# An MLP backward kernel: derivative operations placed one by one by a plan with a clock per engine, a denser warm-up, a tail split over two engines, and thirty extra matmuls at the end

## The chip, the cores and the metric

One core of a Trainium2 chip. The metric is the device time of one execution in microseconds (us); lower is better. A run is repeated, and the runs of the kernel before are taken on the same chip, in the same rounds. The profile is one execution. Its span is about 2 us shorter than the timed figure.

Names: PE is TensorE (matmul), PEld its weight load, DVE VectorE, ACT ScalarE, POOL GpSimd, SP SyncE, which issues most DMAs here. A name with a q (ACTq, SPq) is the sequencer that issues DMAs. The granted clock (PEclk in the views) is the share of its full clock that PE is allowed in a stretch of time.

## The reference

```python
# x [1,2048,448], w1 [448,1792], b1, w2 [1792,448], b2, grad_out [1,2048,448]; all bf16
def fwd(x, w1, b1, w2, b2):
    h = gelu_tanh(x @ w1 + b1)
    return h @ w2 + b2
out, vjp = jax.vjp(fwd, x, w1, b1, w2, b2)
return out, *vjp(grad_out)          # out, dx, dw1, db1, dw2, db2
```

The kernel does this in four stages. With z = x @ w1 + b1:

1. **Forward**: 28 steps (4 blocks of 512 rows, 7 column pairs each). A step has a first product (8 matmuls, z into PSUM), an evacuation pair on ScalarE (gelu into `hT`, a copy of z into `Z`), and a second product (8 matmuls from `hT`, out into four PSUM banks).
2. **Gradient of w2**: 14 groups of 16 matmuls, each evacuated by ScalarE into `gw2_t`.
3. **Backward**: again 28 steps. The evacuation, on VectorE, multiplies by the derivative of gelu, which must stand in `Z` by then.
4. **Gradient of w1**: dense matmuls, little else.

The derivative of gelu is elementwise work on `Z`, 28 pairs of tiles of 128x1024: s (square), v (polynomial), tanh on ScalarE, y, n, and E, the sum. It fills the gaps of VectorE and ScalarE in stages 1 to 3. In the *early* form y uses `hT` while it is still there; in the *late* form `hT` is gone, and s and one more square run on ScalarE.

## The kernel before

The queue of an engine is worked off in the order in which instructions were emitted. `Background` decides that order for the derivative work by credit: each step grants each engine some microseconds, and operations are emitted while credit lasts.

```python
class Background:
    def step(self, dve, act):
        for e, c in (("V", dve), ("A", act)):
            self.credit[e] = min(self.credit[e] + c, 4.0)
        ...  # while anything moved:
        for e in ("V", "A"):
            q = self.ops[e]
            if q and self.credit[e] > 0 and (q[0][3] is None or q[0][3] in self.done):
                cost, fn, tag, _ = q.pop(0)
                fn()                     # emits the instruction(s)
                self.credit[e] -= cost
                self.done.add(tag)       # "done" means emitted
```

A tanh may therefore be emitted in the same step as the v that it reads.

```python
# forward, step p (cut)
pair_mms(ps, w1_sb, xq, fts)                                  # first product
nc.scalar.activation(out=hT[:], in_=ps[:], func=ACT.Gelu_apprx_tanh)
nc.scalar.activation(out=Z[b][...], in_=ps[:], func=ACT.Identity)
chain_step(accs[pb], hist[p - 1], w2_sb, pc)                  # second product of step p-1
if pc == NPAIR - 1:
    out_rows(pb, accs[pb], out2, True)                        # o_blk: 4 additions on VectorE
    dve -= 2.8
bg.step(dve, STEP - 2.16)
...
# gradient of w2 (cut)
gw2_t = tmp.tile([P, 2, D], BF16, name="gw2_t")               # two buffers
nc.scalar.copy(out=gw2_t[:, h, :], in_=ps_w[:, 0:D])
bg.step(3.03, 3.03 - 0.55)                                    # one per 16 matmuls of 3.03 us
...
# backward, step p (cut)
nc.vector.scalar_tensor_tensor(out=ghT[:, h, :], in0=Z[b][:, ft, :], ..., in1=ps[:, h, :], ...)
chain_step(accs[pb], hist[p - 1], w1T_sb, pc)
```

Of the kernel before, what the change touches and what calls it, by code (L numbers as in the profile page):

```python
# [19 lines left out]
def kernel(  # L20
# [49 lines left out]
    class Background:  # L70
        def __init__(self):
            self.ops = {"V": [], "A": []}
            self.done = set()
            self.credit = {"V": 0.0, "A": 0.0}

        def add(self, eng, cost, fn, tag=None, after=None):
            self.ops[eng].append((cost, fn, tag, after))

        def step(self, dve, act):
            for e, c in (("V", dve), ("A", act)):  # L80
                self.credit[e] = min(self.credit[e] + c, 4.0)
            moved = True
            while moved:
                moved = False
                for e in ("V", "A"):
                    q = self.ops[e]
                    if q and self.credit[e] > 0 and (q[0][3] is None or q[0][3] in self.done):
                        cost, fn, tag, _ = q.pop(0)
                        fn()
                        self.credit[e] -= cost  # L90
                        self.done.add(tag)
                        moved = True

        def need(self, tag):
            while tag not in self.done and (self.ops["V"] or self.ops["A"]):
                self.step(1.0, 1.0)

    bg = Background()

    def emit_E(b, c, hT, k, prevs, s_on_act):  # L100
        zc = Z[b][:, 2 * c:2 * c + 2, :]
        t = {}

        def new(nm):
            t[nm] = tmp.tile([P, 2, SB], BF16, name=nm)
            return t[nm]

        def s_():
            s = new("s")
            if s_on_act:  # L110
                nc.scalar.activation(out=s[:], in_=zc, func=ACT.Square)  # L111
            else:
                nc.vector.tensor_tensor(out=s[:], in0=zc, in1=zc, op=ALU.mult)

        def u_():
            v = new("v")
            nc.vector.tensor_scalar(out=v[:], in0=t["s"][:], scalar1=GELU_A, scalar2=1.0, op0=ALU.mult, op1=ALU.add)  # L117
            nc.vector.tensor_tensor(out=v[:], in0=v[:], in1=zc, op=ALU.mult)  # L118

        def tanh_():  # L120
            nc.scalar.activation(out=t["v"][:], in_=t["v"][:], func=ACT.Tanh, scale=GELU_C)  # L121

        def y_():
            y = new("y")
            f = 2.0 if hT is not None else 1.0
            nc.vector.tensor_scalar(out=y[:], in0=t["s"][:], scalar1=f * 3.0 * GELU_A * GELU_C, scalar2=f * GELU_C, op0=ALU.mult, op1=ALU.add)
            nc.vector.tensor_tensor(out=y[:], in0=y[:], in1=zc if hT is None else hT[:], op=ALU.mult)

        def sq_():
            n = new("n")  # L130
            nc.scalar.activation(out=n[:], in_=t["v"][:], func=ACT.Square)  # L131

        def E_():
            if hT is None:
                n = t["n"]
                nc.vector.tensor_scalar(out=n[:], in0=n[:], scalar1=-1.0, scalar2=1.0, op0=ALU.mult, op1=ALU.add)
            else:
                n = new("n")
                nc.vector.tensor_scalar(out=n[:], in0=t["v"][:], scalar1=-1.0, scalar2=1.0, op0=ALU.mult, op1=ALU.add)
            nc.vector.tensor_tensor(out=t["y"][:], in0=t["y"][:], in1=n[:], op=ALU.mult)  # L140
            nc.vector.tensor_tensor(out=zc, in0=t["y"][:], in1=t["v"][:], op=ALU.add)

        if s_on_act:
            bg.add("A", 1.09, s_, ("s", k))
        else:
            bg.add("V", 0.69, s_, ("s", k))
        bg.add("V", 1.12, u_, ("u", k), ("s", k))
        bg.add("A", 1.09, tanh_, ("t", k), ("u", k))
        if hT is None:
            bg.add("A", 1.09, sq_, ("q", k))  # L150
        bg.add("V", 1.12, y_, ("y", k), ("u", k))
        prevs.append((1.81, E_, ("E", b, c), ("q", k) if hT is None else ("t", k)))
        while len(prevs) > 1:
            cost, fn, tag, after = prevs.pop(0)
            bg.add("V", cost, fn, tag, after)
# [19 lines left out]
    pw = [psum_acc.tile([P, SB], F32, name="acc") for _ in range(3)]  # L175
    for i in range(5):
        nc.tensor.matmul(pw[0][:], lhsT=warm[:, 0:P], rhs=warm[:, 0:SB], start=True, stop=True)
    H = P // 2
    for i in range(3):
        for r in range(2):  # L180
            rs = slice(r * H, (r + 1) * H)
            nc.tensor.matmul(pw[1 + r][:, 0:256], lhsT=warm[rs, 0:P], rhs=warm[rs, 0:256], start=True, stop=True)
    for i in range(2):
        for r in range(2):
            rs = slice(r * H, (r + 1) * H)
            for q in range(2):
                nc.tensor.matmul(pw[1 + r][q * H:(q + 1) * H, 0:256], lhsT=warm[rs, q * H:(q + 1) * H], rhs=warm[rs, 0:256],
                                 start=True, stop=True, skip_group_check=True)
# [39 lines left out]
    def out_rows(b, acc, dst, with_b2):  # L228
        blk = tmp.tile([P, SPB, D], BF16, name="o_blk", tag="rows")
        for j in range(SPB):  # L230
            if with_b2:
                nc.vector.tensor_tensor(out=blk[:, j, :], in0=acc[j][:, 0:D], in1=b2_bc[:], op=ALU.add)  # L232
            else:
                nc.scalar.mul(out=blk[:, j, :], in_=acc[j][:, 0:D], mul=0.5)  # L234
        nc.gpsimd.dma_start(out=dst[b * SB:(b + 1) * SB, :].rearrange("(j p) d -> p j d", p=P), in_=blk[:])  # L235

# [4 lines left out]
    STEP = 3.24  # L241
    g_all = big.tile([P, NS, D], BF16, name="g_all", tag="nat_d")
    steps = [(b, c) for b in range(NB) for c in range(NPAIR)]
    late = []
    prevs = []
    accs = {}
    hist = []
    for p in range(len(steps) + 1):
        if p < len(steps):
# [5 lines left out]
            pair_mms(ps, w1_sb, xq, fts)  # L255
            hT = tmp.tile([P, 2, SB], BF16, name="hT", bufs=6)
            nc.scalar.activation(out=hT[:], in_=ps[:], func=ACT.Gelu_apprx_tanh)  # L257
            transpose_out(h_nat, hT, b, fts)
            nc.scalar.activation(out=Z[b][:, 2 * c:2 * c + 2, :], in_=ps[:], func=ACT.Identity)
# [4 lines left out]
            hist.append(hT)  # L264
        dve = STEP
        if p > 0:
            pb, pc = steps[p - 1]
            if pc == 0:
                accs[pb] = [psum_acc.tile([P, SB], F32, name="acc") for _ in range(SPB)]
            chain_step(accs[pb], hist[p - 1], w2_sb, pc)  # L270
            if pc == NPAIR - 1:
                out_rows(pb, accs[pb], out2, True)
                dve -= 2.8
            if pc % 2 == 0:
                emit_E(pb, pc, hist[p - 1], p - 1, prevs, False)
            else:
                late.append((pb, pc))
        bg.step(dve, STEP - 2.16)

# [8 lines left out]
    for k, (b, c) in enumerate(late):  # L288
        emit_E(b, c, None, 100 + k, prevs, True)
    if prevs:  # L290
        bg.add("V", *prevs.pop(0))
# [16 lines left out]
    for st in range(1, NS):  # L308
        bg.add("V", 0.65, lambda st=st: gsum_op(st), ("gsum", st))

    out4_v = out_4.rearrange("(ft p) d -> p ft d", p=P)
    for c in range(NPAIR):
        gw2_t = tmp.tile([P, 2, D], BF16, name="gw2_t")
        for h in range(2):
            ft = 2 * c + h
            ps_w = psum_acc.tile([P, 512], F32, name="acc")
            for st in range(NS):
                nc.tensor.matmul(ps_w[:, 0:D], lhsT=h_nat[:, st, ft * P:(ft + 1) * P], rhs=g_all[:, st, :],  # L318
                                 start=(st == 0), stop=(st == NS - 1))
            nc.scalar.copy(out=gw2_t[:, h, :], in_=ps_w[:, 0:D])  # L320
            bg.step(3.03, 3.03 - 0.55)
# [3 lines left out]
    hist = []  # L325
    for p in range(len(steps) + 1):
        if p < len(steps):
# [4 lines left out]
            bg.need(("E", b, c))  # L332
            ps = psum_z.tile([P, 2, SB], F32, name="ps")
            pair_mms(ps, w2T_sb, gq, fts)
            ghT = tmp.tile([P, 2, SB], BF16, name="hT", bufs=6)
            for h, ft in enumerate(fts):
                nc.vector.scalar_tensor_tensor(out=ghT[:, h, :], in0=Z[b][:, ft, :], scalar=1.0, in1=ps[:, h, :], op0=ALU.add, op1=ALU.mult,  # L337
                                               accum_out=gb1_p[:, b, ft:ft + 1])
            transpose_out(gh_nat, ghT, b, fts)
            if c == 1 and b + 1 < NB:  # L340
                gq_n = load_T(g2, b + 1, "gT_q")
            hist.append(ghT)
        if p > 0:
# [3 lines left out]
            chain_step(accs[pb], hist[p - 1], w1T_sb, pc)  # L347
            if pc == NPAIR - 1:
                out_rows(pb, accs[pb], gx2, False)
        bg.step(STEP - 1.4, STEP - 0.5)  # L350
    assert not bg.ops["V"] and not bg.ops["A"]
# [19 lines left out]
    for cp in range(NCH // 2):  # L371
# [19 lines left out]
        nc.scalar.mul(out=tl[:], in_=ps_w[:, 0:CW], mul=0.5)  # L391
        for h in range(2):
            cs = slice((2 * cp + h) * CW, (2 * cp + h + 1) * CW)
            nc.sync.dma_start(out=out_2[(KD - 1) * P:D, cs], in_=tl[h * DL:(h + 1) * DL, :])


# [28 lines left out]
```

## Time and profile before

| | before |
|---|---|
| time, median | 298.11 us (3 runs, 297.99 to 298.87) |
| span of the profiled run | 295.5 us |
| PE busy | 276.4 us, 94% |
| VectorE, ScalarE busy | 175.9 us, 128.1 us |

PE is the bottleneck, so the question is where it idles or runs slowly. The profile page gives the first hint: the busy tenths of PE, and of its granted clock, in 40 slices of the span.

```profile
PE   7999979989998999998955999999999999999994
PEclk9999999999999999999995999999999999999999
```

Slices 21 and 22 (148 to 163 us, the start of backward) are about half empty, and slice 22 also has a lower clock. The timeline of PE gives sizes. Its columns are start, duration, engine and line, operation, how many, and in brackets the idle time just before and what ended it.

```profile
5.57 5.66 PE L163 MATMUL ps<-xT_q,w_sb 128*128 128x512 bf16 x16 [0.72 <-DMA xT_q<-in_x_dram]
37.45 1.69 PE L170 MATMUL acc<-w_sb,hT 128*128 128x448 bf16 x8 [0.30 <-ACT hT L257]
42.10 1.69 PE L170 MATMUL acc<-w_sb,hT 128*128 128x448 bf16 x8 [1.23 <-ACT hT L257]
...
135.82 12.27 PE L318 MATMUL acc<-g_all,h_nat 128*128 128x448 bf16 x64 [1.12 <-ACT gw_t L320]
158.76 3.17 PE L170 MATMUL acc<-w1T_sb,hT 128*128 128x448 bf16 x8 [7.22 <-DVE hT L337]
```

Read from the top: the first 16 matmuls take 5.66 us (16 of the same kind take 3.62 us at 147.92); twice in each of three blocks PE waits for ScalarE's gelu evacuation; it waits twice (0.19 and 1.12 us) for a bank that ScalarE should have emptied; and it waits 7.22 us for VectorE when backward starts, after which 8 matmuls take 3.17 us instead of the usual 1.68.

Why the evacuation was late: ScalarE's timeline around the first block boundary (L121 is tanh, L257 gelu, L259 the copy of z).

```profile
35.43 1.06 ACT L121 ACTIVATE v<-v 128x1024 bf16<-128x1024 bf16 x1 [2.78 <-DVE v L118]
36.39 1.00 ACT L257 ACTIVATE hT<-ps 128x1024 bf16<-128x1024 f32 x1
37.30 1.01 ACT L259 ACTIVATE Z_103<-ps 128x1024 bf16<-128x1024 f32 x1
40.08 1.06 ACT L121 ACTIVATE v<-v 128x1024 bf16<-128x1024 bf16 x1 [1.76 <-DVE v L118]
41.04 1.00 ACT L257 ACTIVATE hT<-ps 128x1024 bf16<-128x1024 f32 x1
```

Tanh stood at the head of the queue for 2.78 us, waiting for VectorE, and the gelu that PE needed stood behind it. The Trainium skill, "TensorE: Matmul & The Clock Gate", Part 1 (Engine queue depths), calls these queues "strict FIFO"; this trace agrees: the gelu at 36.39 starts as the tanh ends (35.43 plus 1.06 us), though its input had been ready since about 33.9.

Why VectorE was late in backward: VectorE's timeline just before its first evacuation (L337).

```profile
152.63 0.43 DVE L117 TENSOR_SCALAR v<-s 128x1024 bf16<-128x1024 bf16 x1 [0.30 <-ACT s L111]
156.94 0.43 DVE L117 TENSOR_SCALAR v<-s 128x1024 bf16<-128x1024 bf16 x1 [0.30 <-ACT s L111]
157.40 0.69 DVE L118 TENSOR_TENSOR v<-v,Z_105 128x1024 bf16<-128x1024 bf16 x1
158.01 0.68 DVE L337 SCALAR_TENSOR_TENSOR hT<-Z_102,ps 128x512 bf16<-128x512 bf16 x1
```

One derivative pair takes 4.31 us here (156.94 minus 152.63), and the first evacuation, whose input had been ready since about 150 us, stands behind them.

The end of the span: the last real matmuls, the last evacuation and its two DMA issues.

```profile
288.20 3.22 PE L388 MATMUL acc<-gh_nat,x_all 128*64 128x448 bf16 x32
291.51 0.54 ACT L391 ACTIVATE gw_tail<-acc 128x448 bf16<-128x448 f32 x1 [2.66 <-PE acc L388]
292.08 1.11 SPq L394 DMA_DIRECT2D out_dram<-gw_tail  x2
```

### The profile page before, as it was taken

The numbers are of one execution on the slowest core, as the hardware profiler recorded it, in microseconds if no ns is written. First come the engines' busy times: TensorE is split into PE (matmuls) and PEld (weight loads), VectorE is DVE, ScalarE is ACT, GpSimd is POOL, SyncE is SP. The second block draws the span as 40 slices with busy tenths as digits, with TensorE's granted clock in tenths as the row PEclk, the third lists the DMA queues.
The fourth block names the chain that finished last, engine by engine and source line by source line (L and its number), as shares of the span: only waits on it lengthen the run. The fifth ranks groups of instructions, "written<-read, shape, count | busy, mean of one in ns | idle before, by whom it ended". The sixth has DMA issues, their size and how long they took to land.

```text
span 295.5 us, 3804 instructions
## 1 busy us (share of the span) xinstructions
PE 276.4 (94%) x1396; PEld 133.3 (45%) x1396; DVE 175.9 (60%) x362; ACT 128.1 (43%) x153; POOL 22.0 (7%) x31
## 2 busy tenths in 40 slices
PE   7999979989998999998955999999999999999994
PEld 2444434434443455544522444444444444555552
DVE  1366799599599799859999889933433442000000
ACT  1677478568749738669887202002002002211211
POOL 0002100100010011200000001061000001000000
PEclk9999999999999999999995999999999999999999
DMA  7997967576453499941003654869775664211111
GB/s 200 318 162 186 272 122 111 106 151 126 92 133 71 91 170 236 209 84 63 31 31 69 124 105 93 169 115 289 164 120 106 152 91 106 78 49 31 35 45 31
DMA packets 99844, 36.46 MB, mean 123 GB/s; under 512 B 92145, under 2 KB 97889, under 8 KB 99826
## 3 DMA queue, kind: packets, MB, share of 16 engines
q1 hardware_dynamic: 96352, 26.81, 48.0%
q0 software_dynamic: 2512, 8.95, 10.1%
q10 hardware_dynamic: 962, 0.46, 0.6%
q8 instruction: 11, 0.18, 0.3%
q14 instruction: 7, 0.06, 0.1%
HBM read 7.00 MB, written 6.89 MB: 47 GB/s over the span
## 4 chain that ended last, share of the span: by engine, by line
PE 69%; ACT 9%; DVE 9%; DMA 8%; issue 3%; SPq 1%; POOL 1%; ACTq 0%; POOLq 0%; DVEq 0%
PE ps L163 27%; PE acc L170 25%; PE acc L378 12%; DMA out_dram<-gw_t 3%; ACT v L121 3%; DVE v L118 2%; ACT s L111 2%; DVE o_blk L232 2%; PE acc L388 2%; PE acc L318 2%; DVE v L117 2%; ACT hT L257 2%; DMA h_nat<-hT 2%; DMA xT_q<-in_x_dram 2%; DMA w2T_sb<-in_w_dram 2%
## 5 line engine op out<-in xcount | busy, mean ns | idle before, releaser
L170 PEld LDWEIGHTS <-hT 128*128 128x128 bf16 x448 | 43.6, 99 | 58.1 <-DVE hT L337 7.7
L163 PE MATMUL ps<-xT_q,w_sb 128*128 128x512 bf16 x224 | 54.8, 390 | 0.7 <-DMA xT_q<-in_x_dram 0.7
L170 PE MATMUL acc<-w1T_sb,hT 128*128 128x448 bf16 x224 | 48.3, 360 | 7.2 <-DVE hT L337 7.2
L163 PE MATMUL ps<-gT_q,w2T_sb 128*128 128x512 bf16 x224 | 53.6, 383 | 0.0
L170 PE MATMUL acc<-w_sb,hT 128*128 128x448 bf16 x224 | 46.8, 353 | 4.5 <-ACT hT L257 4.5
L318 PE MATMUL acc<-g_all,h_nat 128*128 128x448 bf16 x224 | 42.9, 352 | 1.3 <-ACT gw_t L320 1.3
L121 ACT ACTIVATE v<-v 128x1024 bf16<-128x1024 bf16 x28 | 29.6, 1058 | 32.1 <-DVE v L118 32.1
L234 ACT ACTIVATE o_blk<-acc 128x448 bf16<-128x448 f32 x16 | 7.4, 550 | 72.8 <-issue 40.0
L378 PE MATMUL acc<-gh_nat,x_all 128*128 128x448 bf16 x192 | 36.8, 353 | 0.0
L163 PEld LDWEIGHTS <-w_sb 128*128 128x128 bf16 x224 | 22.4, 100 | 27.5 <-issue 3.6
L257 ACT ACTIVATE hT<-ps 128x1024 bf16<-128x1024 f32 x28 | 28.5, 1018 | 13.9 <-PE ps L163 13.7
L163 PEld LDWEIGHTS <-w2T_sb 128*128 128x128 bf16 x224 | 22.2, 99 | 25.9 <-issue 1.5
L318 PEld LDWEIGHTS <-h_nat 128*128 128x128 bf16 x224 | 21.9, 98 | 22.1 <-issue 1.8
L378 PEld LDWEIGHTS <-x_all 128*128 128x128 bf16 x192 | 18.6, 98 | 17.6 <-issue 0.4
L140 DVE TENSOR_TENSOR y<-y,n 128x1024 bf16<-128x1024 bf16 x28 | 19.4, 692 | 1.0
L382 ACT ACTIVATE gw_t<-acc 128x448 bf16<-128x448 f32 x12 | 6.5, 543 | 29.9 <-PE acc L378 27.6
L337 DVE SCALAR_TENSOR_TENSOR hT<-Z_104,ps 128x512 bf16<-128x512 bf16 x14 | 9.1, 685 | 13.6 <-PE ps L163 13.6
L337 DVE SCALAR_TENSOR_TENSOR hT<-Z_105,ps 128x512 bf16<-128x512 bf16 x14 | 9.1, 685 | 13.5 <-PE ps L163 13.5
L117 DVE TENSOR_SCALAR v<-s 128x1024 bf16<-128x1024 bf16 x28 | 12.9, 461 | 7.0 <-ACT s L111 6.3
L235 POOL DMA_DIRECT2D out_dram<-o_blk x8 | 6.1, 761 | 129.3 <-ACT o_blk L234 75.6
L232 DVE TENSOR_TENSOR o_blk<-acc,b_bc 128x448 bf16<-128x448 f32 x16 | 8.9, 617 | 10.7 <-PE acc L170 10.7
L131 ACT ACTIVATE n<-v 128x1024 bf16<-128x1024 bf16 x12 | 12.7, 1057 | 0.4
(70 smaller groups left out, 208.9 us busy)
## 6 DMA issues: line engine op xcount, KB each, us to landing
out_dram<-o_blk POOLq DMA_DIRECT2D x8, 448.0 KB, 3.9
g_all<-in_grad_out_dram POOLq DMA_DIRECT2D x1, 1792.0 KB, 10.2
x_all<-in_x_dram POOLq DMA_DIRECT2D x1, 1792.0 KB, 9.8
out_dram<-gw_t POOLq DMA_DIRECT2D x7, 224.0 KB, 2.5
out_dram<-gw_t SPq DMA_DIRECT2D x12, 112.0 KB, 1.7
w_sb<-in_w_dram SPq DMA_DIRECT2D x1, 896.0 KB, 6.9
h_nat<-hT SPq DMA_TRANSPOSE x56, 2.5
gh_nat<-hT SPq DMA_TRANSPOSE x56, 2.5
```

The source lines that it names most:

```text
L117: nc.vector.tensor_scalar(out=v[:], in0=t["s"][:], scalar1=GELU_A, scalar2=1.0, op0=ALU.mult, op1=ALU.add)
L121: nc.scalar.activation(out=t["v"][:], in_=t["v"][:], func=ACT.Tanh, scale=GELU_C)
L131: nc.scalar.activation(out=n[:], in_=t["v"][:], func=ACT.Square)
L140: nc.vector.tensor_tensor(out=t["y"][:], in0=t["y"][:], in1=n[:], op=ALU.mult)
L163: nc.tensor.matmul(ps[:, h, :], lhsT=lhs[:, kt, ft * P:(ft + 1) * P], rhs=rhs[:, kt, :], start=(kt == 0), stop=(kt == KD - 1))
L170: nc.tensor.matmul(acc[j][:, 0:D], lhsT=lhs[:, h, j * P:(j + 1) * P], rhs=w[:, ft, :], start=(ft == 0), stop=(ft == NF - 1))
L232: nc.vector.tensor_tensor(out=blk[:, j, :], in0=acc[j][:, 0:D], in1=b2_bc[:], op=ALU.add)
L234: nc.scalar.mul(out=blk[:, j, :], in_=acc[j][:, 0:D], mul=0.5)
L257: nc.scalar.activation(out=hT[:], in_=ps[:], func=ACT.Gelu_apprx_tanh)
L318: nc.tensor.matmul(ps_w[:, 0:D], lhsT=h_nat[:, st, ft * P:(ft + 1) * P], rhs=g_all[:, st, :], start=(st == 0), stop=(st == NS - 1))
L337: nc.vector.scalar_tensor_tensor(out=ghT[:, h, :], in0=Z[b][:, ft, :], scalar=1.0, in1=ps[:, h, :], op0=ALU.add, op1=ALU.mult, accum_out=g ...
L378: nc.tensor.matmul(ps_w[:, 0:CW], lhsT=x_all[:, st, kt * P:(kt + 1) * P], rhs=gh_nat[:, st, cs], start=(st == 0), stop=(st == NS - 1))
```

## The change

Intent: emit each derivative operation alone, in a gap that ends before the next due evacuation, by a plan that keeps one clock per engine; and warm PE up with denser work. The core of the diff, cut:

```diff
-    class Background:            # credit per step
+    class Plan:
+            self.t = {"P": 6.0, "A": 6.0, "V": 6.0}      # a clock per engine
+            self.end, self.bg, self.due = ...            # end times by tag; waiting ops; when the next evacuation is due
+        def fill(self):
+            while True:
+                # among the ops whose inputs have a planned end: the earliest start,
+                # if it also ends by the time the engine's next evacuation is due
+                if k and k[0] + self.bg[e][k[1]][0] <= self.due[e] and (...):
+        def fg(self, eng, cost, fn, tag=None, after=0.0, slack=0.3):
+            if eng != "P":
+                self.due[eng] = after + slack
+                self.fill()
+            fn()
+            self.t[eng] = max(self.t[eng], after) + cost
...
-        bg.add("V", 1.12, u_, ("u", k), ("s", k))        # two VectorE instructions in one entry
+        plan.add("V", 0.44, u_, ("u1", k), (("s", k),))  # one instruction per entry
+        plan.add("V", 0.70, u2_, ("u", k), (("u1", k),))
...
-            if pc % 2 == 0:      # 16 early pairs, 12 late ones
-                emit_E(pb, pc, hist[p - 1], p - 1, prevs, False)
+            open_ = [e for e in early if ("y",) + e not in plan.end]
+            if len(open_) < 3:   # as many early pairs as get through: 18, and 10 late ones
+                early.append((b, c))
+                emit_E(b, c, hT)
...
-    for i in range(5):           # warm-up: 5 full matmuls, then 6 and 8 on part of the array
-        nc.tensor.matmul(pw[0][:], lhsT=warm[:, 0:P], rhs=warm[:, 0:SB], start=True, stop=True)
-    ...
+    for i in range(10):          # 10 full matmuls
+        nc.tensor.matmul(pw[:], lhsT=warm[:, 0:P], rhs=warm[:, 0:SB], start=True, stop=True)
...
         tl = tmp.tile([P, CW], BF16, name="gw1_tail", tag="rows")
-        nc.scalar.mul(out=tl[:], in_=ps_w[:, 0:CW], mul=0.5)
         for h in range(2):
-            nc.sync.dma_start(out=out_2[(KD - 1) * P:D, cs], in_=tl[h * DL:(h + 1) * DL, :])
+            if h == 0:
+                nc.scalar.mul(out=tl[hs, :], in_=ps_w[hs, 0:CW], mul=0.5)
+                nc.scalar.dma_start(out=out_2[(KD - 1) * P:D, cs], in_=tl[hs, :])
+            else:
+                nc.vector.tensor_scalar(out=tl[hs, :], in0=ps_w[hs, 0:CW], scalar1=0.5, ...)
+                nc.sync.dma_start(out=out_2[(KD - 1) * P:D, cs], in_=tl[hs, :])
+    # after everything: 30 matmuls on half the rows, in pairs, into banks that nothing reads
+    for lo, ro, acc_ in ((0, 0, 0), (0, 0, 1), (0, 1, 0), (1, 0, 0), (1, 1, 1)):
+        for i in range(3):
+            for r, bank in enumerate((pa, pb_)):
+                nc.tensor.matmul(bank, lhsT=x_all[HS[r], ...], rhs=gh_nat[HS[r], ...], ...)
```

The work on the data is the same, apart from two pairs that change from the late to the early form.

## The prediction

> **What bounds it.** TensorE. The page gives PE 94% busy; the span is 295.5 us (298.1 us timed). I read PE's losses from its timeline, idle intervals and matmuls slower than steady state (8 first-product matmuls 1.73 us, 8 second-product ones 1.51 us, so 3.24 us a step):
>
> - Start: the first 16 real matmuls take 5.66 us, not 3.46: 2.2 us lost.  The Trainium skill, "TensorE: Matmul & The Clock Gate", Part 1, says the array is at half clock until about 3.4 us of sustained work fill a free-running window. The warm-up of before is thin (small tiles) and leaves 0.72 us idle.
> - Forward: six waits of PE for the hT evacuation on ScalarE, 0.3 and 1.23 us per block boundary, 4.5 us in all, and 1.1 us of restarts. The chain of waits names the cause: o_blk on VectorE holds up v, tanh heads ScalarE's queue waiting for v (2.75 us), and the evacuation stands behind tanh.
> - w2 gradient: 1.3 us of waits for free banks.
> - Backward start: PE idles 7.22 us (151.5 to 158.8) since VectorE still works off derivative operations, then 2.4 us more at granted clock 0.5. Together 9.6 us.
>
> Sum: 18.9 us. Without it the matmuls need about 267 us of the 285.9 between first and last.
>
> **What the change does.** The built order shows tanh no longer ahead of an evacuation it would delay: after each o_blk three evacuation pairs precede the next tanh. 18 pairs instead of 16 take the cheap form, so Square runs on ScalarE 10+10 times instead of 12+12. The gsum additions (15 x 0.65 us) move from before the first backward evacuation to the third backward block. VectorE's total, about 176 us, hardly changes; it is full in forward but no longer blocks PE.
> Warm-up: 10 full matmuls, at the trace's cold rate (about 0.43 us) 1.2 to 5.5 us, just up to x's arrival at 5.57, dense.
> Tail: two evacuations and two DMA issues in parallel save one issue, 0.55 us. The 30 probe matmuls after the last real one use half the rows; if pairs overlap, as the six half-row warm-up matmuls of before did (0.82 us, 1.28 if serial), 15 x 0.22 = 3.3 us fits under the 3.6 us of evacuation and output DMA; if they don't, 6.5 us, costing 3.
> x_all's load now starts after gsum, about 7 steps (24 us) before it is needed; 2.9 us reduction and 9.8 us landing fit.
>
> **Sum.** Start -1.7, forward -5.0, w2 gradient -1.0, backward start -9.2, tail -0.4: -17.3 us. Predicted 280.8 us, 8 in 10 between 278.8 and 283.8; faster by over 2% 0.97, within 2% 0.02, slower 0.01.
>
> **What would show it.** Chain of waits almost wholly PE; PE idle before hT waits under 1 us in forward; no idle over 1 us at backward start and no 0.5 clock there; first 16 matmuls at 3.5 to 4.5 us; gw_t waits for its DMA (3.9 us) may stay, as the slow first output behind the w2T memset is unchanged, and delay the derivative chain by up to 8 us, which four banks and VectorE's slack should absorb. Last matmul to end of span: about 3.6 us.
>
> **What would make it wrong.** That 8 us delay, unknown to the plan, could leave 1 to 4 us idle at backward start; probe pairs may serialise (+3); x_all may arrive late; the clock window's phase moves the start by 1 us.

## The result

| | before | changed |
|---|---|---|
| time, median | 298.05 us (4 runs, 296.38 to 298.87) | 282.0 us (4 runs, 281.53 to 284.11) |
| span of the profiled run | 295.5 us | 280.1 us |
| PE busy | 94% | 98% |

The ratio is 0.9482, with a 95% interval from 0.9419 to 0.9546. Ratios here are the mean time of one kernel's fast runs over that of the other's of the same rounds, so not quite the ratio of the medians that are quoted.

PE's slices on the page of the changed kernel are full from the third to the last but one; the page has no clock row, since no change of clock was recorded.

```profile
PE   7799999999999999999999999999999999999998
```

All the idle times of PE that its timeline lists (line numbers are those of the changed file: L200 is the first product, L207 the second, L214 the warm-up):

```profile
1.21 4.45 PE L214 MATMUL acc<-warm 128*128 128x512 bf16 x10 [1.21 <-DVE warm L211]
5.87 2.40 PE L200 MATMUL ps<-xT_q,w_sb 128*128 128x512 bf16 x8 [0.20 <-DMA xT_q<-in_x_dram]
9.04 0.82 PE L200 MATMUL ps<-xT_q,w_sb 128*128 128x512 bf16 x3 [0.77 <-DMA w_sb<-in_w_dram]
10.99 1.25 PE L200 MATMUL ps<-xT_q,w_sb 128*128 128x512 bf16 x5 [1.13 <-DMA w_sb<-in_w_dram]
```

After 11 us the timeline lists nothing: no wait for gelu, for a bank, or for VectorE. (It leaves out the shortest ones; the page has 0.1 us before L354, the gradient of w2, which matters in experiment 6.) At the first block boundary ScalarE now reads (L154 tanh, L298 gelu, L300 the copy of z):

```profile
31.72 1.02 ACT L298 ACTIVATE hT<-ps 128x1024 bf16<-128x1024 f32 x1 [0.36 <-PE ps L200]
32.64 1.02 ACT L300 ACTIVATE Z_92<-ps 128x1024 bf16<-128x1024 f32 x1
34.96 1.02 ACT L298 ACTIVATE hT<-ps 128x1024 bf16<-128x1024 f32 x1 [1.30 <-PE ps L200]
...
40.02 1.06 ACT L154 ACTIVATE v<-v 128x1024 bf16<-128x1024 bf16 x1
```

Gelu waits for PE, and not PE for gelu; the next tanh comes three evacuation pairs later, without waiting. VectorE's first backward evacuation now waits for PE as well:

```profile
143.95 0.69 DVE L382 SCALAR_TENSOR_TENSOR hT<-Z_91,ps 128x512 bf16<-128x512 bf16 x1 [1.87 <-PE ps L200]
```

The tail of the changed kernel: last real matmuls, the extra ones (L448) and the two evacuations.

```profile
272.66 3.22 PE L429 MATMUL acc<-gh_nat,x_all 128*64 128x448 bf16 x32
275.81 3.41 PE L448 MATMUL ps<-gh_nat,x_all 64*128 64x512 bf16 x30
275.97 0.54 ACT L436 ACTIVATE gw_tail<-acc 64x448 bf16<-64x448 f32 x1 [2.66 <-PE acc L429]
276.54 0.63 DVE L439 TENSOR_SCALAR gw_tail<-acc 64x448 bf16<-64x448 f32 x1 [20.79 <-ACT gw_tail L436]
```

VectorE's half waits for ScalarE's half, so they do not run side by side.

Where the time came from, by stage, from the starts of the first matmul of each stage in the two timelines. (The second product's first matmul ends "start"; the last boundary is the end of the last real matmul, 291.44 and 275.88 us in the chain of waits, the profile's view that follows the work that ended last back through what released each step.)

| stage | before | changed | difference | predicted |
|---|---|---|---|---|
| start, up to the first second product | 11.07 | 12.08 | +1.0 | -1.7 |
| rest of forward | 92.84 | 87.26 | -5.6 | -5.0 |
| gradient of w2 | 44.01 | 42.68 | -1.3 | -1.0 |
| backward | 100.36 | 90.72 | -9.6 | -9.2 |
| gradient of w1 | 43.16 | 43.14 | 0.0 | |
| last real matmul to end of span | 4.06 | 4.22 | +0.2 | -0.4 |
| span | 295.5 | 280.1 | -15.4 | -17.3 |

The three stages in the middle came as predicted. The start and the tail did not, and both got slower instead of faster. So there were two questions for experiments: which part of the plan earns the 16 us, and what holds the start and the tail.

### The profile page after: what moved, and what is told of

Same layout as the page of the kernel before. It is cut to its first block, busy times and chain, and to the rows that moved or that the text cites. A ratio compares the mean times of both kernels' runs of the same rounds, so it can differ in the third digit from the quotient of the medians.

```text
span 280.1 us, 3825 instructions
## 1 busy us (share of the span) xinstructions
PE 274.9 (98%) x1400; PEld 134.5 (48%) x1417; DVE 170.4 (61%) x366; ACT 124.5 (44%) x149; POOL 22.0 (8%) x31
## 4 chain that ended last, share of the span: by engine, by line
PE 89%; DMA 8%; SPq 1%; POOL 1%; issue 0%; ACT 0%; ACTq 0%; POOLq 0%
PE ps L200 33%; PE acc L207 30%; PE acc L419 13%; PE acc L354 9%; DMA w_sb<-in_w_dram 3%; DMA out_dram<-gw_t 3%; PE acc L429 2%; DMA w2T_sb<-in_w_dram 2%; PE ps L448 1%; SPq L318 1%; POOL w2T_sb L320 1%; ACT gw_t L356 0%; ACTq L224 0%; PE ps L406 0%; POOLq L320 0%
## 5 line engine op out<-in xcount | busy, mean ns | idle before, releaser
L207 PEld LDWEIGHTS <-hT 128*128 128x128 bf16 x448 | 43.8, 98 | 43.8
L200 PE MATMUL ps<-xT_q,w_sb 128*128 128x512 bf16 x216 | 52.8, 382 | 2.4 <-DMA w_sb<-in_w_dram 1.9
L200 PE MATMUL ps<-gT_q,w2T_sb 128*128 128x512 bf16 x215 | 52.0, 379 | 0.5
L207 PE MATMUL acc<-w_sb,hT 128*128 128x448 bf16 x224 | 46.8, 352 | 0.1
L207 PE MATMUL acc<-w1T_sb,hT 128*128 128x448 bf16 x224 | 46.8, 352 | 0.0
L354 PE MATMUL acc<-g_all,h_nat 128*128 128x448 bf16 x224 | 42.7, 352 | 0.1
L154 ACT ACTIVATE v<-v 128x1024 bf16<-128x1024 bf16 x28 | 29.6, 1059 | 21.5 <-DVE v L151 21.4
L298 ACT ACTIVATE hT<-ps 128x1024 bf16<-128x1024 f32 x28 | 28.7, 1024 | 22.5 <-PE ps L200 18.1
L200 PEld LDWEIGHTS <-w_sb 128*128 128x128 bf16 x224 | 21.9, 99 | 28.6 <-DMA w_sb<-in_w_dram 2.9
L200 PEld LDWEIGHTS <-w2T_sb 128*128 128x128 bf16 x224 | 21.9, 98 | 25.0
L354 PEld LDWEIGHTS <-h_nat 128*128 128x128 bf16 x224 | 21.9, 98 | 20.8 <-issue 0.4
L439 DVE TENSOR_SCALAR gw_tail<-acc 64x448 bf16<-64x448 f32 x2 | 1.3, 628 | 39.6 <-ACT gw_tail L436 39.6
L148 DVE TENSOR_SCALAR v<-s 128x1024 bf16<-128x1024 bf16 x28 | 12.2, 434 | 8.2 <-ACT s L144 7.8
L356 ACT CAST gw_t<-acc 128x448 bf16<-128x448 f32 x14 | 7.2, 532 | 21.7 <-PE acc L354 12.5
L382 DVE SCALAR_TENSOR_TENSOR hT<-Z_94,ps 128x512 bf16<-128x512 bf16 x14 | 9.1, 685 | 12.4 <-PE ps L200 12.4
L170 DVE TENSOR_SCALAR n<-v 128x1024 bf16<-128x1024 bf16 x18 | 8.9, 493 | 12.2 <-ACT v L154 12.2
```

The source lines that it names most:

```text
L148: nc.vector.tensor_scalar(out=v[:], in0=t["s"][:], scalar1=GELU_A, scalar2=1.0, op0=ALU.mult, op1=ALU.add)
L154: nc.scalar.activation(out=t["v"][:], in_=t["v"][:], func=ACT.Tanh, scale=GELU_C)
L170: nc.vector.tensor_scalar(out=n[:], in0=src[:], scalar1=-1.0, scalar2=1.0, op0=ALU.mult, op1=ALU.add)
L200: nc.tensor.matmul(ps[:, h, :], lhsT=lhs[:, kt, ft * P:(ft + 1) * P], rhs=rhs[:, kt, :], start=(kt == 0), stop=(kt == KD - 1))
L207: nc.tensor.matmul(acc[j][:, 0:D], lhsT=lhs[:, h, j * P:(j + 1) * P], rhs=w[:, ft, :], start=(ft == 0), stop=(ft == NF - 1))
L298: h_end[p] = plan.fg("A", 1.05, lambda: nc.scalar.activation(out=hT[:], in_=ps[:], func=ACT.Gelu_apprx_tanh), after=m1_end + LAT)
```

## The experiments

Twelve kernels, all with correct results. Times are medians of all runs; each ratio is against the kernel before in the same rounds and leaves slow runs out. The kernel before had 299.42 us in the rounds of the first four (7 runs, three of them slow; 298.47 without these), 297.71 in those of the next four (11 runs, two slow; 297.35 without) and 298.51 in those of the last four (11 runs, none slow). The three sets ran on three chips. The record calls the class of each of the first four runs "unclear", so what is read from those four rests on their traces as much as on their ratios.

### 1. Only the place of tanh (b_lag)

On the kernel before: a tanh may be emitted only if its v was emitted in an earlier step, in forward alone.

```diff
+            old = set(self.done)          # what was emitted before this step
-                    if q and self.credit[e] > 0 and (q[0][3] is None or q[0][3] in self.done):
+                    if q and self.credit[e] > 0 and (q[0][3] is None or q[0][3] in (old if self.lag and e == "A" else self.done)):
...
+    bg.lag = False                        # after forward
```

> The kernel before, with one rule added in the forward stage: a tanh may be emitted only in the step after the one that emitted its input v, so at least one more evacuation pair stands ahead of it. Theory (tanh waiting at the head of ScalarE's queue causes the forward stalls): PE waits for hT in forward fall from 4.5 us to under 1 us, their 1.1 us of restarts go as well, the backward start keeps its idle time of about 7 us; 298.0 becomes about 292.5 (ratio 0.98). Rival (the forward stalls come from VectorE being full, and will return wherever tanh stands): PE waits of 3 us or more stay in forward, ratio 0.99 to 1.0.

Measured: 294.93 us, ratio 0.9898 (0.9833 to 0.9962). The forward waits are gone altogether, as the theory has it: the next idle time of PE after the start comes at 123 us. The sum is not what I expected. PE's timeline at the start of backward:

```profile
142.34 3.62 PE L165 MATMUL ps<-gT_q,w2T_sb 128*128 128x512 bf16 x16
155.83 3.17 PE L172 MATMUL acc<-w1T_sb,hT 128*128 128x448 bf16 x8 [9.88 <-DVE hT L340]
```

Backward's first matmul is 5.6 us earlier than before (147.92), but VectorE was not freed by as much, so the idle time there grew from 7.22 to 9.88 us. Nearly half of what forward won was handed to the next wait.

### 2. Only the place of the first backward evacuation (b_credit)

On the kernel before: less credit for VectorE during the gradient of w2, so that 22 pairs stand ahead of the first evacuation instead of 25. No operation changes.

```diff
-            bg.step(3.03, 3.03 - 0.55)
+            bg.step(2.15, 3.03 - 0.55)
```

> The kernel before, with VectorE's credit per half pair of the w2 gradient cut from 3.03 to 2.15, so that 22 derivative pairs instead of 25 stand in VectorE's queue ahead of the first backward evacuation; same work, same form, other place. Theory (place, not amount, causes the idle time at the start of backward): the idle time of 7.2 us and the half clock after it vanish, ratio 0.968 (about 288.5). Rival (VectorE or the pair chain is simply behind): the wait returns in the first two backward blocks where the same pairs come due, ratio 0.985 or more.

Measured: 288.37 us, ratio 0.9671 (0.9612 to 0.9731). This is the theory's number, and the wait for VectorE did not come back: in backward PE's timeline lists only this, after the first block.

```profile
174.61 2.41 PE L170 MATMUL acc<-w1T_sb,hT 128*128 128x448 bf16 x8 [0.66 <-ACT o_blk L234]
```

The same work in another place is worth 9.8 us by the ratio and 8.3 us in the profiled runs (spans of 295.5 and 287.2 us). VectorE was not too slow for its work; three pairs too many stood ahead of the one instruction that PE needed.

### 3. Both together (b_lag_credit)

> Both edits on the kernel before. Theory (the two stalls are separate and local, and the plan with clocks adds nothing else of size): savings add up, 5.5 plus 9.6, about 283 us, ratio 0.949, the time of the changed kernel. Rival (18 cheap pairs, single operations in gaps and the interleaving matter by themselves): 286 us or more, ratio 0.96 or more.

Measured: 284.17 us (283.5 to 284.39), ratio 0.9525 (0.9474 to 0.9575). Two local edits to the kernel before, without a plan, without single operations and with 16 early pairs, reach all but about 2 us of the changed kernel (1.9 us between the profiled spans; the intervals of the two ratios overlap). My expectation was 283 us, 0.949; the measured value lies between the two theories. The traces show what is missing. Both kernels reach the first second product at 12.08 us. Then:

```profile
123.96 3.19 PE L321 MATMUL acc<-g_all,h_nat 128*128 128x448 bf16 x16 [0.24 <-ACT gw_t L323]
127.37 15.29 PE L321 MATMUL acc<-g_all,h_nat 128*128 128x448 bf16 x80 [0.22 <-ACT gw_t L323]
169.46 2.40 PE L172 MATMUL acc<-w1T_sb,hT 128*128 128x448 bf16 x8 [0.66 <-ACT o_blk L236]
```

The first matmul of the gradient of w1 starts at 234.78 us here and at 232.74 in the changed kernel, 2.04 us apart. The three waits (1.1 us) and the 0.7 us by which the last line's eight matmuls exceed their usual 1.68 make up 1.8 of those 2 us. All three lines wait for a ScalarE evacuation. Which ingredient of the plan removes them (single operations, due times, or the 18 early pairs) was not separated.

### 4. Was a slow DMA the root of the late VectorE? (b_bufs)

On the kernel before, four `gw2_t` buffers. With two, ScalarE waits 3.9 us for the first output of this stage to land, and VectorE 3.4 us for ScalarE.

```diff
-        gw2_t = tmp.tile([P, 2, D], BF16, name="gw2_t")
+        gw2_t = tmp.tile([P, 2, D], BF16, name="gw2_t", bufs=4)
```

> The kernel before, with four gw2_t buffers instead of two, so ScalarE no longer waits 3.9 us for the slow first output of the w2 gradient and VectorE no longer 3.4 us for s. Theory (25 pairs ahead of the first backward evacuation are too many even so): the idle time at the start of backward falls from 7.2 to about 3.8 us, with or without the half clock after it; the waits of 1.3 us for banks go; ratio 0.975 to 0.985. Rival (this wait is the root of the late VectorE): the idle time vanishes, ratio 0.965 or less.

Measured: 295.59 us, ratio 0.9929 (0.9851 to 1.0007). The waits for banks went, so PE reached backward 1.3 us earlier (146.58), and the wait for VectorE only fell to 6.23 us:

```profile
156.43 3.17 PE L170 MATMUL acc<-w1T_sb,hT 128*128 128x448 bf16 x8 [6.23 <-DVE hT L337]
```

The rival (this DMA is the root) is out. The theory's direction holds, its size was too large: VectorE came 2.3 us earlier, not 3.4. Its pairs keep their spacing of 4.31 us even when ScalarE does not wait, because VectorE itself is busy for about 4.0 of these.

### 5 to 7. The start: warm-up against load order (a_oldwarm, a_load, a_load_oldwarm)

The changed kernel's warm-up worked as such: its ten matmuls and the first three real ones are about 0.4 us apart, and from 7.03 us on (5.8 us after the first) the real ones run at the short spacing, about 0.22 us. But PE then waits for w1 (0.77 and 1.13 us in the timeline above). I took two edits. One puts the old warm-up back. The other moves columns 256 to 511 of w1 to the queue that loads x, right behind x:

```diff
-    load_w1(nc.scalar, 256, 512)
+    load_w1(nc.sync, 256, 512)
     load_w2(nc.sync, 0, 2)
     load_w1(nc.sync, 512, 1024)
```

On the other queue the issue of these two pieces waited for the landing of earlier ones (in the changed kernel they were issued at 3.97 and 5.62 us). The Trainium skill, "DMA: Bandwidth & Descriptors", section "Queues, rings and completion order", says that within a queue, on each DMA engine, descriptors are consumed in ring order; so what is issued first on the busy queue should be served first. The outcome agrees: in a_load the two pieces were issued at 3.57 and 4.20 us and landed 3.1 and 2.7 us later, while in the changed kernel the second one took 5.3 us.

> The changed kernel with the warm-up of before. Theory W (at the start the third and fourth pieces of w1, which land near 11 us, bound the first 16 matmuls once PE is warm, so the longer warm-up only turns half clock into waiting): same time as the changed kernel within 0.6 us, first second-product matmul at 11 to 12.2 us. Rival, the step of the prediction (the warm-up saves 1.7 us): 1.7 us slower than the changed kernel, 283.7 against 282.0.

> The changed kernel with w1 columns 256 to 511 issued on the queue of x, right behind x and ahead of w2 and the rest of w1, instead of on the other queue where the issue waits for an earlier landing. Theory W: the waits of PE for w1 (1.9 us) go, the first second-product matmul starts 1.5 to 2 us earlier than 12.1, about 280.3 us, ratio 0.943. Rival (the DMA engines are full until 11 us, whatever the order): within 0.5 us of the changed kernel.

> The same load order with the warm-up of before. Theory W: now that w1 is early, the clock bounds the start, and the old warm-up costs 1 to 2 us against the new load order with the new warm-up. Rival (the warm-up is worth nothing in any case): same within 0.5 us.

The first entry is from the changed kernel's own rounds, the other three share their rounds. Times are medians of all runs; one of a_load's six is slow (285.51), and its fast ones alone have 280.83.

| | warm-up new | warm-up old |
|---|---|---|
| old load order | 282.0 us, 0.9482 (changed kernel) | 281.87 us, 0.9480 (a_oldwarm) |
| new load order | 281.46 us, 0.9448 (a_load) | 282.81 us, 0.9502 (a_load_oldwarm) |

First, with the old load order the new warm-up is worth nothing that shows. The two ratios agree, though their intervals (0.9419 to 0.9546 and 0.9444 to 0.9516) alone would not exclude 1.7 us; the traces decide. The first second product starts at 12.08 us with the new and at 12.23 with the old one, and both wait for the same piece of w1, to 10.99 (above) and to 11.14 us (a_oldwarm):

```profile
11.14 1.25 PE L200 MATMUL ps<-xT_q,w_sb 128*128 128x512 bf16 x5 [1.02 <-DMA w_sb<-in_w_dram]
```

That is where the predicted 1.7 us went: the faster clock only makes PE wait for the next piece.

Second, the new load order does move the start: the first second product begins at 9.66 us instead of 12.08 in the profiled run, with no wait for w1 listed:

```profile
5.62 4.20 PE L200 MATMUL ps<-xT_q,w_sb 128*128 128x512 bf16 x16
```

Yet the whole kernel gained only about 1 us (fast runs: 280.83 against a_oldwarm's 281.87), and the profiled run, one of the two longer fast ones, only 0.2 us of span against the changed kernel's. PE's timeline of a_load shows where 2.35 of the 2.4 us went in it, and the chain of waits (start, duration, what) leads there:

```profile
106.19 1.32 SPq L318
107.55 4.90 DMA w2T_sb<-in_w_dram
112.58 1.53 POOL w2T_sb L320
114.12 8.85 DMA out_dram<-gw_t
```

```profile
123.65 18.32 PE L354 MATMUL acc<-g_all,h_nat 128*128 128x448 bf16 x96 [2.35 <-ACT gw_t L356]
```

The load of w2 transposed, the memset on POOL behind it, and the first `gw2_t` output behind that on POOL's queue are a chain that hardly moves with PE's start: that output lands at 123 us in the changed kernel too. There PE waits only about 0.1 us for the bank, yet the chain of waits of the changed kernel already runs through it:

```profile
114.49 8.69 DMA out_dram<-gw_t
123.86 18.32 PE acc L354 x96
```

So the changed kernel had no slack left here. Whoever makes its PE faster before 123 us runs into this limit, and the 1.7 us forecast for the start would have done so too.

Third, that new wait can also cost the clock. In the profiled run of a_load_oldwarm it was 2.10 us, and PE's clock halved right after it (columns of the windows: stretch, length, PE busy and count, granted clock, DMA share, GB/s):

```profile
120.00:122.00 2.00, 1.57 (x9) 1.00 1.15 241
122.00:124.00 2.00, 0.34 (x2) 0.93 1.34 173
124.00:126.00 2.00, 2.00 (x7) 0.50 0.80 186
```

In a_load's profiled run a wait of 2.35 us at the same place was not followed by it. The Trainium skill, "TensorE: Matmul & The Clock Gate", Part 1, describes a free-running window of about 3.4 us. The recorded stretch at half clock lasted 3.41 us, one such window; why the shorter wait was enough and the longer one was not, no run here shows. Three of a_load_oldwarm's six runs had a mean clock of 0.994, as one such stretch would give, and those are its longer ones (283.69 to 285.06 against 281.21 to 281.94; all six count as fast), so this table alone does not say what the warm-up is worth. All twelve runs of experiments 9 and 10, which remove this wait, had 1.000.

### 8. All at once, and no faster (a_best)

The changed kernel with the new load order, the two tail halves in tiles of their own, and without the extra matmuls.

> The changed kernel with the new load order, the two last tail evacuations in tiles of their own (VectorE's no longer waits for ScalarE's), and without the 30 probe matmuls. Expected: start minus 1.7, tail minus 0.5 to 0.6, probe 0.0 since it ends 0.9 us before the span: 279.7 us, ratio 0.940; from last real matmul to the end 3.6 us instead of 4.2. If the probe does cost something, more than that.

Measured: 282.02 us (281.15 to 284.2), ratio 0.9486 (0.9446 to 0.9527), no faster than the changed kernel. Two expectations fell. The start was early (first second product at 9.27 us), but it ran into the wait of experiment 6 (1.49 us, and 0.56 for a later piece of w1). And tiles of their own for the outputs did not part the two evacuations:

```profile
275.18 0.54 ACT L436 ACTIVATE gw_tail<-acc 64x448 bf16<-64x448 f32 x1 [2.61 <-PE acc L429]
275.75 0.63 DVE L439 TENSOR_SCALAR gw_tail<-acc 64x448 bf16<-64x448 f32 x1 [20.79 <-ACT gw_tail L436]
```

What they still share is the PSUM bank that they read.

### 9 and 10. Removing the limit behind the start (a_lb, a_lb_oldwarm)

The changed kernel with the new load order and four `gw2_t` buffers, so that ScalarE need not wait for the slow first output; with the new and with the old warm-up.

> The changed kernel with the new load order and four gw2_t buffers. Theory G (the 2.4 us won at the start in the earlier run of the new load order were given back in the w2 gradient, where PE waited 2.35 us at 123.7 us for a bank that ScalarE could not empty before the first gw_t output had landed, at a time that the DMA queue sets): the wait goes, the first second-product matmul stays at 9.4 to 9.9 us, 279.4 us, ratio 0.9395. Rival (some other limit of the DMA queue stands behind it): a wait of 1.5 us or more shows up at the start of backward or later, no faster than 281.

> The same with the warm-up of before. If the clock bounds the start once the w1 pieces are early, 1 to 2 us slower than the run with the new warm-up; if the warm-up is worth nothing even then, within 0.5 us of it.

| | time, all six runs | ratio |
|---|---|---|
| a_lb | 279.25 us (278.87 to 279.59) | 0.9357 (0.9323 to 0.9391) |
| a_lb_oldwarm | 280.58 us (279.15 to 281.32) | 0.9391 (0.9352 to 0.9430) |

Theory G holds: the wait is gone, the first second product starts at 9.08 us, and the win of the start reaches the end, but for one new wait for gelu of 0.45 us at 42.09 us in a_lb's profiled run. The buffer count that could not be told from nothing on the kernel before (0.9929, up to 1.0007), where VectorE held PE anyway, is worth 0.9% here (ratio 0.9448 without, 0.9357 with it, in different rounds and on another chip).

Now the warm-up can be judged. With the old one two runs are as fast as with the new (279.15 and 279.16), and four lie at 280.48 to 281.32; with the new all six are within 0.72 us. The difference of the medians is 1.3 us, close to the 1.7 that I had predicted for the changed kernel, where it was zero. The intervals of the two ratios overlap, so the size is uncertain. That the slower four lost it to the half clock at the start is likely but not shown: the only one of these runs with a profile is one of the two fast ones.

### 11 and 12. The tail and the extra matmuls (a_best2, a_best2_probe)

As a_lb, with the two halves of the tail in PSUM banks of their own as well; without and with the extra matmuls.

```diff
-        ps_w = psum_acc.tile([P, 512], F32, name="acc")
+        ps_t = [psum_acc.tile([P, 512], F32, name="acc") for _ in range(2)]
...
-                nc.scalar.mul(out=tl[hs, :], in_=ps_w[hs, 0:CW], mul=0.5)
+                nc.scalar.mul(out=tl[hs, :], in_=ps_t[h][hs, 0:CW], mul=0.5)   # and the same on VectorE
```

> New load order, four gw2_t buffers, the two halves of the last tail in PSUM banks and tiles of their own, no probe matmuls. ScalarE and VectorE now both wait for PE alone, so the halves are evacuated at the same time: last real matmul to end 3.5 us instead of 4.1; 278.8 us, ratio 0.9375. If the two evacuations again stand one after the other, 279.4.

> The same with the 30 probe matmuls kept. They take 3.4 us after the last real matmul and the output takes 3.5: same time within 0.2 us. If they delay the last output or the end of the program: 0.5 us or more slower.

Measured: a_best2 278.68 us (278.51 to 279.29), ratio 0.9343 (0.9309 to 0.9377), the fastest kernel; a_best2_probe 279.42 us (279.22 to 279.6), ratio 0.9362 (0.9325 to 0.9399). The two evacuations of a_best2 now start together, each on PE alone:

```profile
273.30 0.54 ACT L436 ACTIVATE gw_tail<-acc 64x448 bf16<-64x448 f32 x1 [2.60 <-PE acc L429]
273.33 0.63 DVE L439 TENSOR_SCALAR gw_tail<-acc 64x448 bf16<-64x448 f32 x1 [20.79 <-PE acc L429]
```

From the last real matmul (273.31 in its chain of waits) to the end of the span (276.9) it is 3.6 us, instead of 4.2 in the changed kernel. My expectation that the extra matmuls cost at most 0.2 us was wrong: they cost 0.7 us in the median and 0.5 us in the profiled spans (the intervals of the ratios overlap). With them in place the split of the banks bought nothing (a_lb 279.25, a_best2_probe 279.42). They lie at the end of the chain of waits of a_best2_probe:

```profile
269.90 3.15 PE acc L429 x32
273.05 3.34 PE ps L448 x30
```

PE is through at 276.39 us, and the span ends at 277.4. The program's end comes about 1 us after its last instruction on PE, which I had left out. In the changed kernel the extra matmuls end at 279.22 and the span at 280.1, by the same rule; there the slow tail of the outputs ends at nearly the same time, so taking them away alone would gain little: in a_best, which has the same serial evacuations and no extra matmuls, it is 4.0 us from the last real matmul to the end of the span, against 4.2. That is an inference: no run took away only them from the changed kernel.

## Why the prediction was right, and where a step was off

The time was predicted as 280.8 us, with a range of 278.8 to 283.8, and 282.0 was measured: right in the range. Point by point:

- **Forward, -5.0 predicted, -5.6 measured: right, with its mechanism.** Tanh at the head of ScalarE's queue was the cause. b_lag moved tanh alone, and the waits vanished.
- **Start of backward, -9.2 predicted, -9.6 measured: right.** But the prediction only said that VectorE was behind, and did not say why the new order would not be. The number followed from assuming that the wait would vanish, so its being right is partly luck. b_credit showed the cause: the number of pairs emitted ahead of the first evacuation (25 against 22), not the amount of work.
- **A misreading on the way.** The prediction said that the gsum additions stood before the first backward evacuation in the kernel before. In the emitted order they stand in its first two backward blocks, so moving them cannot have shortened this wait.
- **The delay by the first gw_t output: right.** ScalarE's wait for it grew to 9.2 us, and four banks and VectorE's slack did absorb it in the changed kernel, but only just: PE waited about 0.1 us. This too was luck: the same forecast counted on a start 1.7 us earlier, and in a_load a start 2.4 us earlier brought the wait back (2.35 us).
- **Start, -1.7 predicted, +1.0 measured: this step failed.** The clock was taken to be the only limit of the first 16 matmuls. The trace of before already listed a wait of 0.3 us of the weight load (PEld) for w1 among them, which said that the pieces landed hardly before they were needed. a_oldwarm and the changed kernel show the two warm-ups equal; a_load and a_lb show that the load order is the first lever; the warm-up is a likely second, about 1.3 us in the medians of a_lb and a_lb_oldwarm. In the profiled runs the last piece also landed later than in before's (about 10.9 against 9.8 us), so the +1.0 is partly scatter of the loads: b_lag_credit, with the old warm-up, also reached the first second product at 12.08 us in its profiled run.
- **Tail, -0.4 predicted, +0.2 measured: this step failed too.** The two evacuations were not parallel, since they shared a PSUM bank; the emitted order with its waits, which could be read without the chip, would have told. That the extra matmuls overlap in pairs was right (30 took 3.41 us, 3.3 forecast), but "fits under the 3.6 us" forgot the end of the program.

In the profiled runs the two failed terms cost 2.7 and 0.6 us and the stages in the middle gave back 1.3, so the saving is about 2 us short of the forecast (15.4 for 17.3); in the medians it is 1.2 us (282.0 for 280.8).

## What to carry to other kernels

Where engines work off their queues in order, what matters is what stands ahead of the instruction that the bottleneck waits for; count it before you make anything faster, since here a change of one constant, moving three pairs behind one evacuation, was worth 3%, over half of the whole change. When a saving is smaller than expected, look for the limit just behind: a kernel that is ahead of its DMA by less than the saving will hand it back, as the warm-up did to the w1 load and the load order to the w2 chain. Cheap edits that showed no clear gain alone can pay once the limit ahead of them is gone: four buffers did (0.9%), and the denser warm-up (1.3 us in the medians) and the split tail without the extra matmuls (0.6 us) probably did.

## What the Trainium skill lacked or had wrong

- "TensorE: Matmul & The Clock Gate", its closing table, advises no idle gaps of PE over about 3 us. In a_load_oldwarm an idle time of 2.10 us was followed by a window of half clock (3.41 us). In a_load a gap of 2.35 us was not. So a shorter gap can be followed by half clock, though not in every run.
- "PSUM — Partial Sum Buffer", section "PSUM bank collisions raise a hardware error", speaks of dependencies by bank and quadrant. In the programs here a ScalarE read of partitions 0 to 63 and a VectorE read of partitions 64 to 127 of one bank were still put one after the other (0.57 us apart); with two banks they started 0.03 us apart. This is how the program was built, not a limit of the chip that these runs show.
- I found no page that says how long after the last matmul the profiled span ends when PE is the last engine at work (the nearest is "Runtime: NRT & Kernel Launch"); it was 0.9 and 1.0 us in the changed kernel and in a_best2_probe.
